# GpSimd's steady share of lower parts and sums given to VectorE in an attention + two-FFN kernel

## The chip, the cores and the metric

The kernel runs on one NeuronCore of a Trainium2 chip. The metric is device time in microseconds: the median of three timed runs. Five engines work side by side, each through its own instructions in the order in which they were written: TensorE (PE, matmul), VectorE (DVE), ScalarE (ACT), GpSimd (POOL) and SyncE (SP, which issues the DMAs here). GpSimd can't read PSUM, where matmuls leave their results; VectorE and ScalarE can.

## The reference

```python
def _attn_ref(q, k, v, mem_k, mem_v):          # 4 batches, 8 heads, 768 tokens, head_dim 64
    ...                                        # chunks of 32 queries see 8 memory keys and
    for c in range(nc):                        # their own window: 16 left, 32, 8 right
        ...
        scores = scale * np.matmul(q_c, k_full.transpose(0, 1, 3, 2))
        scores = scores - np.max(scores, axis=-1, keepdims=True)
        a = np.exp(scores)
        a = a / (np.sum(a, axis=-1, keepdims=True) + 1e-09)
        out[:, :, c_start:c_end] = np.matmul(a, v_full)
def _moe_ref(x, w_in, w_out):                  # 3072 tokens, 512 -> 2048 -> 512
    h = x @ w_in
    g = h * (1.0 / (1.0 + np.exp(-1.702 * h)))
    return (g @ w_out).astype(np.float32)
def _moe2_ref(x, w_gate, w_val, w_out):        # 512 -> 1536 -> 512
    g = x @ w_gate
    silu = g * (1.0 / (1.0 + np.exp(-g)))
    val = x @ w_val
    return (silu * val @ w_out).astype(np.float32)
```

Windowed attention, then a feed-forward network (FFN 1), then a gated one (FFN 2), all in float32.

## The kernel before

**Splitting.** Each float32 operand of a matmul is held as two numbers: an upper part (rounded to the type that TensorE takes, written by ScalarE: `split_hi`, L255 for weights, L432 for tokens, L561 for hidden values) and a lower part, what the rounding left (`split_lo`, L258 for weights, L436 for tokens, L565 for hidden values). A product is three matmul passes, `PASSES`: upper by upper, upper by lower, lower by upper. A lower part can be made only when its upper part is there.

**Seven products for eight.** A block of 512 tokens by 512 channels and the up-projection's weights are cut into 2 x 2 quarters, and sums of quarters are multiplied so that seven quarter products do for eight. Sums of weight quarters are `first_sums` and `second_sums` (L322, L323, L326, L327, 256 columns each); sums of token quarters are in `Tokens.sum` (L406, L409, L412, L415, 512 columns each). Each sum is then split too.

**Units.** A unit is one step along the hidden dimension for one block of tokens (`unit`, L465). PE runs, in this order: product 0 (into PSUM tile `ps_a`), product 1 (`ps_b`), a chunk of the down-projection of an earlier unit (`y`, L585), product 3 (`ps_a`), product 2 (`ps_c`, or the other half of `ps_b`), chunk 0, product 5 (`ps_a`), chunk 1, product 4 (`ps_c`), chunk 2, product 6 (`ps_a`); product 6 and the next unit's product 0 are neighbours. In FFN 2 a chunk is three matmuls of 512 columns, in FFN 1 six. A product is six matmuls of 256 columns. Between them ScalarE copies (L483, L492, L496) and VectorE adds (L487, L502, L508). After product 4 and L508 the activation of `ps_b` runs on ScalarE (L553 in FFN 2); after product 6 VectorE multiplies (L531 in FFN 2, L557 in part of FFN 1), ScalarE makes the upper part of the hidden values (L561) and VectorE the lower part (L565). Chunk 0 of the next unit reads it, in its second pass. Product 6 writes the PSUM tile that L502 reads and writes.

**Blocks.** There are 24 passes over a block, `seq`: six blocks with the first hidden units of FFN 1, six with the rest, then the same for FFN 2. At a change of block the next block's seven token operands are made during the last two units: `Tokens(..., TE)` has, for each of the 7 splits and 4 sums, the engine that does it. `EARLY`, `LATE` and `MAKE` say after which of the eleven places of a unit each is recorded; under `MAKE` operand 1 is split at place 0, behind product 0. At FFN 1's first five changes attention for the next block runs as well.

**Weights.** A generator, `weight_steps`, makes one unit's weight tiles in steps; `pace` (L954) takes a step or two at the places of a unit, in time for the unit's first use. A step is recorded on the engines at that place, so its instructions stand there in each engine's queue.

**Order.** The program for PE, ScalarE, VectorE and GpSimd runs as recorded (`manual_schedule`); only the order of SP's DMAs is chosen by a scheduler. The first part, up to the third unit of the second block, is an order written out by hand, `OPENING`.

Of the kernel before, what the change touches and what calls it, by code (L numbers as in the profile page):

```python
# [10 lines left out]
F32 = mybir.dt.float32  # L11
# [25 lines left out]
HALF = 2 * P  # L37
# [20 lines left out]
def tile_attention_moe_moe(  # L58
# [8 lines left out]
    nc = tc.nc  # L67
# [178 lines left out]
    def new_w(key):  # L246
        ring = max(rings, key=lambda r: r.room())
        wt[key], wslot[key] = ring.take()
# [5 lines left out]
    def split_hi(w, f, o=0, n=512):  # L254
        nc.scalar.copy(w[:, 0, o : o + n], f)  # L255

    def split_lo(w, f, o=0, n=512):
        nc.gpsimd.tensor_sub(w[:, 1, o : o + n], f, w[:, 0, o : o + n].bitcast(F32))  # L258

    def split_w(*a):  # L260
        split_hi(*a)
        split_lo(*a)

    raws = []
    AT = (0, 1, 4, 5, 2, 3, 6, 7)
# [40 lines left out]
    def next_weights(out):  # L306

        i = nraw[0]
        load_raw(i + RB)
        nraw[0] += 1  # L310
        take_words(i)
        yield 0
        shift_words(i)
        yield 0
        join_words(i)
        out += [bits.pop(i), raws[i]]

    def quarters(raw):
        return raw.bitcast(F32).rearrange("p (s n) -> p s n", s=4)

    def first_sums(s, a, b):
        nc.gpsimd.tensor_add(s[:, 0], b[:, :HALF], b[:, HALF:])  # L322
        nc.gpsimd.tensor_sub(s[:, 1], s[:, 0], a[:, :HALF])  # L323

    def second_sums(s, a, b):
        nc.gpsimd.tensor_sub(s[:, 2], a[:, :HALF], b[:, :HALF])  # L326
        nc.gpsimd.tensor_sub(s[:, 3], a[:, HALF:], s[:, 1])  # L327

    def weight_steps(ph, u):

        yield 0
        t = []
        yield from next_weights(t)
        a = t[0]
        yield 1
        new_w((ph, u, "a"))
        split_w(wt[ph, u, "a"], a)
        yield 0
        t = []
        yield from next_weights(t)  # L340
        b, raw = t
        s = quarters(raw)
        yield 0
        first_sums(s, a, b)
        yield 1 - u % 2
        if u % 2 == 0:
            new_w((ph, u, "v"))
        split_w(wt[ph, u - u % 2, "v"], b[:, HALF:], (u % 2) * HALF, HALF)
        yield 0
        second_sums(s, a, b)  # L350
        for i, n in enumerate(("s12", "s34")):
            yield 1
            new_w((ph, u, n))
            split_w(wt[ph, u, n], s[:, 2 * i : 2 * i + 2].rearrange("p s n -> p (s n)"))
        for o in range(OUTS[ph]):
            yield 0
            t = []
            yield from next_weights(t)
            yield 1
            new_w((ph, u, o))  # L360
            split_w(wt[ph, u, o], t[0])
        ready.add((ph, u))
# [3 lines left out]
    def all_weights():  # L366
        for ph in (1, 2):
            for u in range(2 * PLAIN if ph == 1 else 0, UNITS[ph]):
                yield from weight_steps(ph, u)
        yield None  # L370
# [67 lines left out]
    def load_tokens(src, engs):  # L438
        t = xpool.tile([P, KC, BLK], F32, tag="xf", name="xl")
        nc.sync.dma_start(out=t, in_=src)  # L440
        return Tokens(t, engs)
# [220 lines left out]
    V, G = nc.vector, nc.gpsimd  # L662
# [175 lines left out]
    def tokens():  # L838
# [27 lines left out]
        "ct": join_words,  # L866
        "wa": lambda u: new_split((1, u, "a"), bits[IN[u]]),
        "wal": lambda u: split_lo(wt[1, u, "a"], bits[IN[u]]),
        "sumA": lambda u: first_sums(*sums_of(u)),
        "sumB": lambda u: second_sums(*sums_of(u)),  # L870
        "wv": hi_v,
        "wvl": lambda u: split_v(u, split_lo),
        "wb": split_b,
        "wbl": lambda u: split_lo(wt[1, u, "a21"], bits[IN[u] + 1][:, :HALF], 0, HALF),
# [119 lines left out]
    LATE = {0: (-1, 0), 1: (-2, 1), 2: (-3,), 3: (3, -4), 4: (2,), 5: (5,), 7: (4,), 9: (6,)}  # L994

    pends = [None, None]
    TE = [V, G, V, G, V, G, V, G, V, V, G]
    done = 0
    for n, (ph, b, ua, ub) in enumerate(seq):
        nxt = seq[n + 1] if n + 1 < len(seq) else None  # L1000
# [5 lines left out]
        for u in range(ua, ub):  # L1006
# [4 lines left out]
            if last and attends and n:  # L1011
                tok = Tokens(xf.pop(nxt[1]), TE)
            places = PLACES[u - ua] if n > 1 and attends else ()
# [37 lines left out]
            if u == ua and nxt is not None and not attends:  # L1051
                src = {1: xd, 2: yd}[nxt[0]][nxt[1]]
                tok = load_tokens(src, TE)
            done += 1
# [53 lines left out]
```

## Time and profile before

| | |
|---|---|
| median of 3 runs | 1189.63 us (1189.48 to 1189.91) |
| the profiled execution's own time | 1190.33 us |
| its span in the profile | 1188.6 us |
| PE busy in the span | 97% |
| VectorE, ScalarE, GpSimd busy | 55%, 48%, 30% |

The profiled execution is 0.70 us above the median and 1.7 us longer than its span. Busy time is what the engine's instructions took; an engine that stands at an instruction whose input is not there yet is not busy, and everything behind that instruction waits too.

### The profile page before, as it was taken

To read this page: it belongs to the slowest core of one execution; us is meant where nothing else is said; L and a number is where in the kernel's file an instruction comes from. 1 tells how busy PE (TensorE), PEld (TensorE's weight loads), DVE (VectorE), ACT (ScalarE), POOL (GpSimd) and SP (SyncE) were. 2 spreads that over 40 slices of the span, in tenths; PEclk is the share of its full clock that TensorE was granted. 3 is DMA by queue.
4 is the path that set the end of the run, shared out by engine and by line. 5 is a ranking of instruction groups with operands and counts; after the bars stand their busy time and mean duration, and the time that the engine had idled before them with its cause. 6 is when DMAs were issued, how large, how long until landed. Compare 5 with 4: busy or idle time off the path is not lost.

```text
span 1188.6 us, 22301 instructions
## 1 busy us (share of the span) xinstructions
PE 1151.3 (97%) x8908; PEld 1039.6 (87%) x8908; DVE 652.1 (55%) x1117; ACT 568.1 (48%) x1185; POOL 354.9 (30%) x321
## 2 busy tenths in 40 slices
PE   4889999999999999999999999999999999999998
PEld 3778888888989999999988989999999999999997
DVE  5886756565765444443466564453556554453553
ACT  4866555455565454444455544343445544243342
POOL 4564221202454232321235433021345521021010
PEclk9889999999999999999999999999999999999999
DMA  9977354441454313322333321210225130320302
GB/s 304 296 253 231 110 157 120 130 140 63 137 166 118 106 66 114 131 74 62 106 116 107 106 99 36 72 71 1 89 89 178 36 103 5 107 92 15 107 25 83
DMA packets 62920, 131.47 MB, mean 111 GB/s; under 512 B 5728, under 2 KB 26208, under 8 KB 60512
## 3 DMA queue, kind: packets, MB, share of 16 engines
q1 hardware_dynamic: 62816, 130.05, 34.9%
q8 instruction: 70, 1.15, 0.4%
q14 instruction: 34, 0.28, 0.1%
HBM read 98.57 MB, written 31.46 MB: 109 GB/s over the span
## 4 chain that ended last, share of the span: by engine, by line
PE 86%; DMA 5%; DVE 3%; ACT 2%; issue 2%; POOL 1%; SPq 0%; DVEq 0%; ACTq 0%; POOLq 0%
PE y L585 35%; PE ps_a L450 27%; PE ps_c L450 12%; PE ps_b L450 9%; DMA raw<-in_wr 2%; PE ps_s L201 1%; PE ps_o L174 1%; DMA q<-in_qg 1%; DMA w<-in_kg 1%; DMA xd<-xf 1%; PE ps_t L158 1%; PE ps_v L174 1%; ACT ebd L167 0%; PE ps_u L546 0%; ACT g L551 0%
## 5 line engine op out<-in xcount | busy, mean ns | idle before, releaser
L450 PEld LDWEIGHTS ps_a<-b,w 128*128 128x128 f32 x2832 | 384.3, 189 | 39.6 <-DVE ps_a L502 4.2
L450 PE MATMUL ps_a<-b,w 128*128 128x256 f32 x2832 | 397.5, 283 | 5.7 <-DVE ps_a L502 2.1
L585 PE MATMUL y<-gs,w 128*128 128x512 f32 x1152 | 298.6, 395 | 0.6 <-DVE gs L565 0.5
L585 PE MATMUL y<-w,gs 128*128 128x512 f32 x864 | 247.7, 395 | 0.6 <-DVE gs L565 0.5
L585 PEld LDWEIGHTS y<-gs,w 128*128 128x128 f32 x1152 | 204.2, 189 | 36.2 <-DVE gs L565 1.4
L450 PE MATMUL ps_c<-b,w 128*128 128x256 f32 x1224 | 179.1, 282 | 0.0
L450 PEld LDWEIGHTS ps_c<-b,w 128*128 128x128 f32 x1224 | 167.1, 190 | 8.8
L585 PEld LDWEIGHTS y<-w,gs 128*128 128x128 f32 x864 | 144.2, 190 | 14.4 <-DVE gs L565 1.7
L258 POOL TENSOR_TENSOR w<-wf,w 128x512 fp32r<-128x512 f32 (+1 forms) x68 | 78.3, 1152 | 222.0 <-ACT w L255 221.9
L450 PE MATMUL ps_b<-b,w 128*128 128x256 f32 x900 | 135.5, 287 | 1.7 <-DVE ps_b L821 1.2
L450 PEld LDWEIGHTS ps_b<-b,w 128*128 128x128 f32 x900 | 120.4, 193 | 5.9 <-issue 1.7
L553 ACT ACTIVATE g<-ps_b 128x512 f32<-128x512 f32 x72 | 43.1, 598 | 166.1 <-DVE ps_b L508 166.1
L436 DVE TENSOR_TENSOR b<-xl,b 128x512 fp32r<-128x512 f32 x72 | 64.3, 893 | 80.4 <-ACT b L432 80.3
L502 DVE TENSOR_TENSOR ps_a<-m,ps_a 128x256 f32<-128x256 f32 x115 | 48.9, 426 | 104.0 <-PE ps_a L450 98.0
L492 ACT COPY u<-ps_a 128x256 f32<-128x256 f32 x115 | 43.0, 373 | 107.8 <-PE ps_a L450 107.6
L415 POOL TENSOR_TENSOR xl<-xl,t 128x512 f32<-128x512 f32 x18 | 23.3, 1296 | 231.3 <-DVE t L412 230.0
L565 DVE TENSOR_TENSOR gs<-ps_a,gs 128x512 fp32r<-128x512 f32 x118 | 80.8, 685 | 10.2 <-ACT gs L561 9.8
L487 DVE TENSOR_TENSOR ps_b<-p,ps_b 128x256 f32<-128x256 f32 x115 | 49.2, 427 | 61.3 <-PE ps_b L450 54.0
L561 ACT CAST gs<-ps_a 128x512 fp32r<-128x512 f32 x118 | 69.8, 592 | 22.5 <-DVE ps_a L531 15.6
L531 DVE TENSOR_TENSOR ps_a<-g,ps_a 128x512 f32<-128x512 f32 x72 | 50.0, 694 | 45.7 <-PE ps_a L450 45.2
L483 ACT COPY p<-ps_a 128x256 f32<-128x256 f32 x115 | 43.0, 374 | 60.3 <-PE ps_a L450 56.4
L508 DVE TENSOR_TENSOR ps_b<-u,ps_c 128x256 f32<-128x256 f32 x102 | 43.5, 426 | 50.1 <-PE ps_c L450 49.8
(123 smaller groups left out, 1190.6 us busy)
## 6 DMA issues: line engine op xcount, KB each, us to landing
raw<-in_wr SPq DMA_DIRECT2D x49, 512.0 KB, 3.4
xl<-yd SPq DMA_DIRECT2D x12, 1024.0 KB, 4.8
vm<-in_vg SPq DMA_DIRECT2D x22, 512.0 KB, 6.0
kbd<-in_kg SPq DMA_DIRECT2D x32, 256.0 KB, 4.2
raw<-in_wr SPq DMA_DIRECT2D x30, 256.0 KB, 5.3
yp<-o SPq DMA_DIRECT2D x24, 256.0 KB, 3.8
xl<-xd SPq DMA_DIRECT2D x6, 1024.0 KB, 4.8
base<-yp SPq DMA_DIRECT2D x24, 256.0 KB, 3.4
```

What stands on the lines that cost most here:

```text
L258: nc.gpsimd.tensor_sub(w[:, 1, o : o + n], f, w[:, 0, o : o + n].bitcast(F32))
L436: self.engs[k].tensor_sub(x[:, 1], self.source(k), x[:, 0].bitcast(F32))
L450: nc.tensor.matmul(ps, w[:, a, o + kc * P : o + kc * P + P], x[:, c, kc, :], start=(start and kc == 0 and (a, c) == PASSES[0]), stop=(kc = ...
L483: nc.scalar.copy(p1, ca[:, :n])
L487: add(cb[:, :n], p1, cb[:, :n])
L502: add(ca[:, n:], m, ca[:, :n])
L508: add(cb[:, n:], u2, cc)
L531: late[0] = [lambda: nc.vector.tensor_mul(ca, t, ca), lambda: gs.append(cast(ca))]
L553: nc.scalar.activation(t, c, AF.Silu)
L561: nc.scalar.copy(x[:, 0], g)
L565: nc.vector.tensor_sub(x[:, 1], g, x[:, 0].bitcast(F32))
L585: nc.tensor.matmul(y, lhs, rhs, start=(first and o == 0 and (a, c) == PASSES[0]), stop=(ends and o == len(gs) - 1 and (a, c) == passes[-1]),)
```

## The change

VectorE takes, outside the written first part, the lower parts of weights, the sums of weight quarters, and those token splits and sums that GpSimd had. ScalarE's upper parts stay, and so does the place at which each piece is recorded.

```diff
-    def split_lo(w, f, o=0, n=512):
-        nc.gpsimd.tensor_sub(w[:, 1, o : o + n], f, w[:, 0, o : o + n].bitcast(F32))
+    def split_lo(w, f, o=0, n=512, eng=nc.gpsimd):
+        eng.tensor_sub(w[:, 1, o : o + n], f, w[:, 0, o : o + n].bitcast(F32))
     def split_w(*a):
         split_hi(*a)
-        split_lo(*a)
+        split_lo(*a, eng=nc.vector)
...
-    def first_sums(s, a, b):
-        nc.gpsimd.tensor_add(s[:, 0], b[:, :HALF], b[:, HALF:])
-        nc.gpsimd.tensor_sub(s[:, 1], s[:, 0], a[:, :HALF])
+    def first_sums(s, a, b, eng=nc.gpsimd):
+        eng.tensor_add(s[:, 0], b[:, :HALF], b[:, HALF:])
+        eng.tensor_sub(s[:, 1], s[:, 0], a[:, :HALF])
...
-        first_sums(s, a, b)
+        first_sums(s, a, b, nc.vector)
...
-        second_sums(s, a, b)
+        second_sums(s, a, b, nc.vector)
...
-    TE = [V, G, V, G, V, G, V, G, V, V, G]
+    TE = [V] * 11
```

(`second_sums` gets the same argument as `first_sums`.) 258 instructions move from GpSimd's queue to VectorE's: 84 of L258, 66 of L436, 22 each of L406 and L415, 16 each of L322, L323, L326 and L327. 178 of them have 512 columns and 80 have 256. The orders of PE and of ScalarE are the same as before; a few DMAs of SP change places with their neighbours.

VectorE's queue at a change of block in FFN 2 with no weight step near (`ps_a_10570` is the last unit but one, `ps_b_10677` the last; `b` are token operands):

```order
 L531 TENSOR_TENSOR ps_a_10570<-g_10641,ps_a_10570 128x512
+L436 TENSOR_TENSOR b_10674<-xl_10117,b_10674 128x512
 L487 TENSOR_TENSOR ps_b_10677<-p1_10660,ps_b_10677 128x256
 L565 TENSOR_TENSOR gs_10672<-ps_a_10570,gs_10672 128x512
+L436 TENSOR_TENSOR b_10689<-t2_10621,b_10689 128x512
 L436 TENSOR_TENSOR b_10707<-xl_10117,b_10707 128x512
+L436 TENSOR_TENSOR b_10713<-t3_10600,b_10713 128x512
 L502 TENSOR_TENSOR ps_a_10663<-m_10662,ps_a_10663 128x256
```

The lower part of operand 1 now stands ahead of L487 and L565; those of operands 3 and 5 stand behind L565 and ahead of L502.

VectorE's queue at an earlier change of block in FFN 2, with a weight tile `w` split at the last place of the unit before:

```order
 L508 TENSOR_TENSOR ps_b_7118<-u2_7105,ps_c_7141 128x256
 L301 SCALAR_TENSOR_TENSOR wf_7172<-raw_6966,wf_7172 128x512
+L258 TENSOR_TENSOR w_7197<-wf_7172,w_7197 128x512
 L531 TENSOR_TENSOR ps_a_7107<-g_7185,ps_a_7107 128x512
+L436 TENSOR_TENSOR b_7214<-xl_7006,b_7214 128x512
 L487 TENSOR_TENSOR ps_b_7217<-p1_7200,ps_b_7217 128x256
 L565 TENSOR_TENSOR gs_7212<-ps_a_7107,gs_7212 128x512
```

Here the weight's lower part stands ahead of L531 as well.

VectorE's queue one block later, where one unit's weight sums (in `raw`) and the tiles made of them are recorded:

```order
 L301 SCALAR_TENSOR_TENSOR wf_7282<-raw_7092,wf_7282 128x512
+L322 TENSOR_TENSOR raw_7092<-wf_7282 128x256
+L323 TENSOR_TENSOR raw_7092<-raw_7092,wf_7172 128x256
+L258 TENSOR_TENSOR w_7346<-wf_7282,w_7346 128x256
 L502 TENSOR_TENSOR ps_a_7299<-m_7298,ps_a_7299 128x256
 L609 TENSOR_SCALAR o_7359<-y1_7072 128x512
+L326 TENSOR_TENSOR raw_7092<-wf_7172,wf_7282 128x256
+L327 TENSOR_TENSOR raw_7092<-wf_7172,raw_7092 128x256
 L508 TENSOR_TENSOR ps_b_7310<-u2_7297,ps_c_7330 128x256
+L258 TENSOR_TENSOR w_7373<-raw_7092,w_7373 128x512
+L258 TENSOR_TENSOR w_7388<-raw_7092,w_7388 128x512
 L531 TENSOR_TENSOR ps_a_7299<-g_7371,ps_a_7299 128x512
```

Two sums now stand ahead of L508, and two weight tiles' lower parts between L508 and L531. This piece occurs twice in FFN 2.

## Rows read from the trace of the kernel before

**Rows 1.** Windows: stretch, then busy us (instructions) of PE, PEld, DVE, ACT, POOL.
```profile
620.00:720.00 100.00, 98.58 (x673) 90.14 (x672) 57.23 (x98) 50.69 (x108) 45.47 (x44) 1.00 0.28 98
720.00:880.00 160.00, 160.00 (x1110) 149.34 (x1109) 76.39 (x139) 67.00 (x145) 33.67 (x31) 1.00 0.17 60
...
120.00:1160.00 1040.00, 1034.36 (x7395) 940.39 (x7394) 555.44 (x959) 486.18 (x1018) 292.46 (x257) 1.00 0.30 93
```

**Rows 2.** Timeline, FFN 2 change of block with weights: start, us, engine, line.
```profile
885.77 0.68 DVE L409 TENSOR_TENSOR xl<-xl 128x512 f32<-128x512 f32 x1
...
887.16 1.29 POOL L258 TENSOR_TENSOR w<-wf,w 128x512 fp32r<-128x512 f32 x1 [2.32 <-ACT w L255]
887.21 1.79 DVE L412 TENSOR_TENSOR t<-t,xl 128x512 f32<-128x512 f32 x1
...
888.92 0.41 DVE L502 TENSOR_TENSOR ps_a<-m,ps_a 128x256 f32<-128x256 f32 x1
...
889.39 1.69 PE L450 MATMUL ps_a<-b,w 128*128 128x256 f32 x12 [0.31 <-DVE ps_a L502]
```

**Rows 3.** Timeline, VectorE, at another change of block in FFN 2.
```profile
691.79 1.78 DVE L301 SCALAR_TENSOR_TENSOR wf<-raw,wf 128x512 int32<-128x512 int32 x1
```

**Rows 4.** Timeline of the quiet change of block in FFN 2.
```profile
956.20 0.43 DVE L487 TENSOR_TENSOR ps_b<-p,ps_b 128x256 f32<-128x256 f32 x1 [0.73 <-PE ps_b L450]
956.22 0.64 ACT L432 CAST b<-xl 128x512 fp32r<-128x512 f32 x1
956.54 0.68 DVE L565 TENSOR_TENSOR gs<-ps_a,gs 128x512 fp32r<-128x512 f32 x1
...
956.94 1.30 POOL L436 TENSOR_TENSOR b<-xl,b 128x512 fp32r<-128x512 f32 x1 [2.21 <-ACT b L432]
...
958.07 0.86 PE L585 MATMUL y<-w,gs 128*128 128x512 f32 x3
...
958.77 0.87 PE L450 MATMUL ps_a<-b,w 128*128 128x256 f32 x6
```

**Rows 5.** Timeline, FFN 2: a chunk 0 that waited for L565.
```profile
649.73 0.69 DVE L565 TENSOR_TENSOR gs<-ps_a,gs 128x512 fp32r<-128x512 f32 x1 [0.32 <-ACT gs L561]
649.76 0.48 PE L585 MATMUL y<-w,gs 128*128 128x512 f32 x1
...
651.04 0.86 PE L450 MATMUL ps_a<-b,w 128*128 128x256 f32 x6
```

**Rows 6.** Timeline of a token sum and L565 in FFN 1 with attention.
```profile
176.10 0.69 DVE L409 TENSOR_TENSOR xf<-xf 128x512 f32<-128x512 f32 x1 [1.64 <-DMA xd<-xf]
176.71 0.68 DVE L565 TENSOR_TENSOR gs<-ps_a,gs 128x512 fp32r<-128x512 f32 x1
...
177.45 0.73 PE L585 MATMUL y<-gs,w 128*128 128x512 f32 x2 [0.51 <-DVE gs L565]
```

**Rows 7.** Timeline, FFN 2 change of block with a weight tile.
```profile
639.49 0.62 ACT L255 CAST w<-wf 128x512 fp32r<-128x512 f32 x1
...
641.98 0.86 PE L585 MATMUL y<-w,gs 128*128 128x512 f32 x3
```

**Rows 8.** Timeline, FFN 2: the weight sums and what is made of them.
```profile
653.35 0.43 DVE L508 TENSOR_TENSOR ps_b<-u,ps_c 128x256 f32<-128x256 f32 x1
...
654.30 0.61 ACT L255 CAST w<-raw 128x512 fp32r<-128x512 f32 x1
...
654.82 0.70 DVE L531 TENSOR_TENSOR ps_a<-g,ps_a 128x512 f32<-128x512 f32 x1 [1.04 <-PE ps_a L450]
...
655.30 0.62 ACT L255 CAST w<-raw 128x512 fp32r<-128x512 f32 x1
...
658.11 0.86 PE L585 MATMUL y<-w,gs 128*128 128x512 f32 x3
```

**Rows 9.** Timeline at the change from the first half of FFN 1 to its second.
```profile
324.84 0.60 ACT L551 ACTIVATE g<-ps_b 128x512 f32<-128x512 f32 x1 [4.50 <-DVE ps_b L508]
...
328.15 0.98 PE L450 MATMUL ps_a<-b,w 128*128 128x256 f32 x6 [0.84 <-ACT p L483]
```

More of the change, by code (lines that the diff above doesn't have):

```diff
@@ L319, in quarters, with second_sums @@
         return raw.bitcast(F32).rearrange("p (s n) -> p s n", s=4)
-    def first_sums(s, a, b):
-        nc.gpsimd.tensor_add(s[:, 0], b[:, :HALF], b[:, HALF:])
-        nc.gpsimd.tensor_sub(s[:, 1], s[:, 0], a[:, :HALF])
-    def second_sums(s, a, b):
-        nc.gpsimd.tensor_sub(s[:, 2], a[:, :HALF], b[:, :HALF])
-        nc.gpsimd.tensor_sub(s[:, 3], a[:, HALF:], s[:, 1])
+    def first_sums(s, a, b, eng=nc.gpsimd):
+        eng.tensor_add(s[:, 0], b[:, :HALF], b[:, HALF:])
+        eng.tensor_sub(s[:, 1], s[:, 0], a[:, :HALF])
+    def second_sums(s, a, b, eng=nc.gpsimd):
+        eng.tensor_sub(s[:, 2], a[:, :HALF], b[:, :HALF])
+        eng.tensor_sub(s[:, 3], a[:, HALF:], s[:, 1])
     def weight_steps(ph, u):
```

## The prediction

> **What bounds the kernel now.** I read the windows by stage first. From 120 to 1160 us PE is idle for 1040.00 - 1034.36 = 5.64 us in all [rows 1]. Where few weights are made, from 720 to 880 us, it has no idle time: PE is the floor there, and a faster VectorE buys nothing. So an upper limit on the gain stands at once, about 5.6 us or 0.5%; the downside has no such limit. What idle time there is lies where weights and block changes meet, as from 620 to 720 us (1.42 us), and in the first blocks of FFN 1. The second view is the timeline around those idle times, because PE waits there for one VectorE or ScalarE instruction, and the question for each is what stands ahead of it in its queue.
>
> **Work moved.** GpSimd takes 1.29 us for a lower part of 512 columns, VectorE 0.68 us for the same shape [rows 2], and 0.43 us for 256 columns [rows 4]. The 178 and 80 moved instructions come to 178 x 0.68 + 80 x 0.43 = 155 us, which lifts VectorE from 555 us to at most 710 of 1040 us, 68% [rows 1]. On average that fits. As GpSimd isn't waited for except through its results, its 292 us saved are worth nothing by themselves; what counts is where the 258 instructions stand in VectorE's queue.
>
> **What gets better.** VectorE and GpSimd get in each other's way: L409 took 0.68 us alone, and the like L412 took 1.79 us beside a GpSimd instruction that ran from 887.16 to 888.45 [rows 2]. That made L502 late, and PE waited for it (0.31 us idle at 889.39). With GpSimd silent L412 is 1.1 us shorter; one lower part of 0.60 us takes its place ahead of L502, so L502 ends 0.5 us earlier: gain 0.5. At 691.79 us a contended L301 of 1.78 us stands ahead of another late L502 [rows 3], and one lower part is added: 0.5 again. By the same steps I put the remaining late L502 and L531 of FFN 2 at 0.6 together, since what is added there eats most of the relief. The largest is in FFN 1: contended instructions hold L508 back, ScalarE stands 4.50 us for it, and PE then waits 0.84 us for ScalarE's copy [rows 9]. Without contention L508 comes 1.2 us earlier; the pause and its restart are worth 1.1. Sum of gains 0.5 + 0.5 + 0.6 + 1.1 = 2.7 us; bounds 1 and 5.64.
>
> **What gets worse, 1: quiet block changes of FFN 2.** Before, operand 1's lower part ran on GpSimd at 956.94 while VectorE did L487 and L565 [rows 4]. Now it stands ahead of both, and waits for ScalarE's upper part, which ends at 956.22 + 0.64 = 956.86. Back to back, an instruction of 512 columns holds the next one up by 0.61 us (176.10 to 176.71 [rows 6]), one of 256 columns by 0.34 (956.20 to 956.54 [rows 4]). So L436 starts at 956.86, L487 at 957.47, L565 at 957.81 and ends at 958.49, against 957.22 before. When must it end? At 649 us L565 ended at 650.42, 0.66 us after chunk 0 began, and the next product came 1.28 us after that begin [rows 5] where 0.70 is normal (958.07 to 958.77 [rows 4]): 0.58 us lost, so L565 is free up to 0.08 us behind the chunk's begin. Here it ends 0.42 behind: 0.34 us lost. FFN 2 has eleven block changes; nine look like this one (the one at 688 us too), 9 x 0.33 = 3.0 us. Bounds: 0 where the upper part gets ready 0.34 us sooner, 0.6 if semaphores add half of that again. The operands behind L565 delay L502 by some 0.5 us, which has 1.2 us to spare: nothing.
>
> **Worse, 2: the two other block changes.** Near 640 us a weight tile's lower part stands ahead of L531 too. ScalarE writes its upper part until 639.49 + 0.62 = 640.11 [rows 7]. L531 then starts at 640.7 instead of 639.5; ScalarE's conversion of the hidden values follows at 641.4, operand 1's upper part behind it at about 641.9 to 642.6, its lower part from 642.6, L487 at 643.2, L565 from 643.55 to 644.2. Chunk 0 began at 641.98: 2.1 us late. VectorE's chain ahead of this is up to 0.6 us faster without GpSimd, so 1.5 is my value, with 0.9 and 2.1 as ends. Near 892 us the weight tile stands behind L565 and only operand 1 is ahead; by the same steps 0.7 (0.3 to 1.3), since the chain is later there than in the quiet case.
>
> **Worse, 3: weight sums ahead of L508.** At 653 us L326 and L327 and a late L502 push L508 from 653.35 to about 654.1 [rows 8]. ScalarE's activation follows 0.74 us late, and so do the two upper parts behind it, which ended at 654.91 and 655.92. The second lower part then starts at 656.7, L531 at 657.3 instead of 654.82, the conversion ends at 658.6, L565 at 659.3. Chunk 0 began at 658.11: 1.1 us lost. If ScalarE weren't late, L531 would start at 656.55 and 0.45 would be lost. The pattern comes twice (at 907 us again): 2 x 1.0 = 2.0 us, ends 0.9 and 2.3. Other weight steps stand behind L565, or ahead of L531 with the one unit's slack of about 0.9 us that the quiet case shows between L565's end and chunk 0's begin [rows 4]: nothing, and 0.3 us each for some ten of them if that slack is gone.
>
> **Worse, 4: FFN 1 with attention.** At 176.10 us L409 had waited for a store to DRAM that reads the same tile, L565 stood behind it, and PE behind L565 [rows 6]. Operand 1's lower part now stands between the two: 0.61 us more for PE. This pattern comes twice: 1.2 us, ends 0.6 and 1.3. In the rest of FFN 1 chunks are twice as long and I count nothing.
>
> **Sum.** Costs 3.0 + 1.5 + 0.7 + 2.0 + 1.2 = 8.4 us, gains 2.7, net +5.7 us. The profiled execution would go from 1190.33 to about 1196.0 us; it stands 0.70 above the median, so the median goes from 1189.63 to **1195.3 us**.
>
> **Rivals.** No difference is what lies within 0.2%, or 2.4 us: about what a measurement of this kernel can tell.
>
> *Relief wins (faster).* Every idle time of PE that contention causes goes, and the new waits are shorter than I work out, because ScalarE, too, gets its inputs earlier. For it speaks that the sums were on the path of the upper parts made from them; against it, that the quiet change has no contention ahead of it and still comes out 0.34 us late. Gains alone: 1189.63 - 2.7 = 1186.9 us; the floor is 1189.63 - 5.64 = 1184.0. It decides if operand 1's lower part is done 0.34 us sooner than I have it. The Trainium skill, "GPSIMD Engine Reference", section "4.1 Engine selection", says that elementwise work on a tile belongs on VectorE, about twice as fast as GpSimd for two inputs. By that rule this change is a gain, and the time would be this rival's 1186.9 us. The trace agrees on the ratio (1.29 to 0.68 us), but not on what follows from it, as GpSimd's speed isn't what PE waits for. Chance 0.07.
>
> *A draw.* The terms with weight tiles (1.5, 0.7 and 2.0) don't appear, since VectorE catches up; the quiet changes and the attention (4.2) stay against gains of 2.7: 1189.63 + 1.5 = 1191.1 us. Chance 0.18.
>
> *ScalarE and VectorE in lockstep (much slower).* Every one of the 84 + 66 lower parts makes VectorE stand until ScalarE's queue has reached its upper part, ScalarE then stands for VectorE's next result, and the slack of ordinary units goes. 84 weight tiles at 0.15 us would add 12.6 us to my sum: 1207.9 us. Against it: VectorE is idle more than 40% of both windows of FFN 2 [rows 1], and most weight steps stand where ScalarE has nothing else ahead. Chance 0.10.
>
> **How the numbers follow.** My forecast (1192 to 1202, around 1195.3) has the remaining 0.65. The range leaves out about one in ten on each side: 1190.0 to 1201.0, from the draw's lower part up to all costs at their upper ends with the gains halved (8.4 + 4 - 1.4 = 11). Faster by over 0.2%: 0.07; within: 0.18; slower: 0.65 + 0.10 = 0.75.
>
> **What would show it.** The profile of the changed kernel has GpSimd idle after about 120 us, VectorE near 66% busy from 120 to 1160 us, and no L409, L412, L301 or L296 above 0.9 us there. PE's new idle time stands at chunk 0 (L585) and is put down to L565: once in each block change of FFN 2, about 0.3 us, and around 1 us at the two units behind the weight sums. The waits of PE for L502 near 692 and 889 us and for the copy near 328 us are gone. I'm wrong if PE's idle time doesn't grow, if it stands ahead of products and not of chunk 0, or if matmuls themselves change pace.

## The result: 0.7% slower, and where it went

The changed kernel takes 1198.78 us (median of 4 runs, 1195.43 to 1200.29) against 1189.77 us before: ratio 1.0069, 95% interval 1.0057 to 1.0082. Ratios are taken from fast runs alone and need not equal the quotient of two medians (1.0076 here); one run each of experiments 6 and 8, with 3762.56 and 1600.19 us, is left out of them. The profiled execution took 1199.83 us, its span is 1198.0 us. The page's busy times and three windows (columns as in [rows 1]):

```profile
PE 1155.7 (96%) x8908; PEld 1040.2 (87%) x8908; DVE 748.2 (62%) x1375; ACT 570.8 (48%) x1185; POOL 59.4 (5%) x63
...
620.00:720.00 100.00, 96.90 (x656) 88.23 (x655) 72.40 (x141) 49.96 (x105) 0.00 (x0) 1.00 0.30 101
720.00:880.00 160.00, 159.68 (x1103) 148.28 (x1103) 89.31 (x167) 66.83 (x142) 0.00 (x0) 1.00 0.17 60
120.00:1160.00 1040.00, 1029.57 (x7341) 933.30 (x7340) 648.24 (x1209) 486.29 (x1015) 0.00 (x0) 1.00 0.29 92
```

PE's idle time in the long window goes from 5.64 us [rows 1] to 10.43, although the matmuls are the same and the granted clock is full (1.00); as the kernel is slower, 54 fewer of them fall into the window. VectorE is busy 648 of 1040 us, 62%: it isn't short of time. PE's own waits from 120 to 1175 us (total, times, longest) say what PE waits for, first in the changed kernel, then in the kernel before:

```profile
PE y L585 <- DVE gs L565: 5.7, 8, 1.7
PE ps_a L450 <- DVE ps_a L502: 1.5, 3, 0.9
PE ps_o L174 <- ACT ebd L167: 1.3, 3, 0.5
...
PE ps_a L450 <- DVE ps_a L502: 2.1, 5, 0.6
...
PE ps_a L450 <- ACT p L483: 1.1, 2, 0.8
PE y L585 <- DVE gs L565: 1.0, 3, 0.5
```

So waits ahead of products shrank (though the longest for L502 grew from 0.59 to 0.92 us, at 960.69 us), those of its matmuls for L483's copy are gone, and the wait of chunk 0 for the hidden values' lower part grew.

To size each place I took, from both traces, the start of product 1 of 116 units from 106 us on, and how much the distance to the kernel before grows from one unit to the next. (The sums of idle time say less than the starts, since the ends of matmuls are modelled and some records are missing.)

| place | predicted | found |
|---|---|---|
| eight quiet block changes of FFN 2 | 8 x 0.33 = 2.6 | 0.35 to 0.39 at seven, 0.55 at one: 3.15 |
| the change near 691 us, and the unit behind it | 0.33 - 0.5 = -0.2 | 0.59 - 0.88 = -0.3 |
| change near 640 us, and the units beside it | 1.5 - 0.6 = 0.9 | 1.94 - 0.30 - 0.56 = 1.1 |
| change near 892 us, and the units beside it | 0.7 - 0.5 = 0.2 | 0.74 - 0.64 - 0.16 = -0.1 |
| weight sums at 655 and 907 us | 2 x 1.0 = 2.0 | 1.33 + 1.32 = 2.65 |
| attention at 176 and 230 us | 2 x 0.6 = 1.2 | 1.15 + 0.30 = 1.45 |
| FFN 1 near 325 us | -1.1 | -0.73 |
| sum | 5.7 | 7.2 |

The distance at the last unit is 9.0 us in these two executions; the spans differ by 9.4, so 0.4 us more stand behind it. Of the 9.0, small steps elsewhere add 0.1, and another 1.7 us stand ahead of the first of these units (106.3 us before, 108.0 now): in the written opening, where every engine's order is the same in both kernels.

The quiet change of block that answers to [rows 4], in the timeline of the changed kernel:

```profile
961.14 0.42 DVE L508 TENSOR_TENSOR ps_b<-u,ps_c 128x256 f32<-128x256 f32 x1
...
963.44 0.62 ACT L432 CAST b<-xl 128x512 fp32r<-128x512 f32 x1
...
964.09 0.69 DVE L436 TENSOR_TENSOR b<-xl,b 128x512 fp32r<-128x512 f32 x1 [1.17 <-ACT b L432]
...
964.70 0.42 DVE L487 TENSOR_TENSOR ps_b<-p,ps_b 128x256 f32<-128x256 f32 x1
965.03 0.69 DVE L565 TENSOR_TENSOR gs<-ps_a,gs 128x512 fp32r<-128x512 f32 x1
965.07 0.39 PE L585 MATMUL y<-w,gs 128*128 128x512 f32 x1
...
965.77 0.73 PE L585 MATMUL y<-w,gs 128*128 128x512 f32 x2 [0.31 <-DVE gs L565]
...
966.35 0.86 PE L450 MATMUL ps_a<-b,w 128*128 128x256 f32 x6
```

VectorE stands 1.17 us idle at L436 until ScalarE's upper part is there, with L487 and L565 behind it. Chunk 0's first pass runs, its second waits. From 965.07 to the next product it is 1.28 us, where 0.70 is normal: 0.58 us. This is the one change of the eight that cost 0.55 from unit to unit. L415, a token sum that ran on GpSimd before, stands ahead of L508 here (960.54 us, 0.69 long), and L508 comes 0.59 us late (961.14, against 953.55 and units that are 7.00 us later). With it ScalarE's upper part comes 0.22 us later than worked out. At the other seven all of the loss, too, stands at chunk 0.

The change of block with a weight tile, which stood near 640 us in the kernel before, in the changed kernel:

```profile
641.47 0.62 ACT L255 CAST w<-wf 128x512 fp32r<-128x512 f32 x1
...
642.12 0.69 DVE L258 TENSOR_TENSOR w<-wf,w 128x512 fp32r<-128x512 f32 x1 [0.69 <-ACT w L255]
...
642.73 0.69 DVE L531 TENSOR_TENSOR ps_a<-g,ps_a 128x512 f32<-128x512 f32 x1
...
644.59 0.69 DVE L436 TENSOR_TENSOR b<-xl,b 128x512 fp32r<-128x512 f32 x1 [1.17 <-ACT b L432]
...
645.53 0.69 DVE L565 TENSOR_TENSOR gs<-ps_a,gs 128x512 fp32r<-128x512 f32 x1
```

Two waits for ScalarE stand one behind the other in VectorE's order, L258's ahead of L531 and L436's ahead of L565. The loss at chunk 0 is 2.0 us. And the unit with the weight sums, which answers to [rows 8]:

```profile
657.02 0.42 DVE L326 TENSOR_TENSOR raw<-wf 128x256 f32<-128x256 f32 x1
657.36 0.42 DVE L327 TENSOR_TENSOR raw<-wf,raw 128x256 f32<-128x256 f32 x1
...
657.69 0.42 DVE L508 TENSOR_TENSOR ps_b<-u,ps_c 128x256 f32<-128x256 f32 x1
658.15 0.60 ACT L553 ACTIVATE g<-ps_b 128x512 f32<-128x512 f32 x1 [2.43 <-DVE ps_b L508]
...
659.28 0.69 DVE L258 TENSOR_TENSOR w<-raw,w 128x512 fp32r<-128x512 f32 x1 [1.17 <-ACT w L255]
...
660.15 0.38 ACT L483 COPY p<-ps_a 128x256 f32<-128x256 f32 x1
660.29 0.69 DVE L258 TENSOR_TENSOR w<-raw,w 128x512 fp32r<-128x512 f32 x1 [0.31 <-ACT w L255]
660.58 0.77 PEld L450 LDWEIGHTS ps_a<-b,w 128*128 128x128 f32 x6 [0.57 <-ACT p L483]
660.90 0.69 DVE L531 TENSOR_TENSOR ps_a<-g,ps_a 128x512 f32<-128x512 f32 x1
...
663.16 0.73 PE L585 MATMUL y<-w,gs 128*128 128x512 f32 x2 [0.41 <-DVE gs L565]
```

L508 is held up 0.67 us by two sums, and L531 by two lower parts that wait for ScalarE. The unit loses at two places. With L508 all of ScalarE's queue is late, L483's copy too, and the weight loads of product 3 wait for that copy: 0.4 us are lost ahead of chunk 0. At chunk 0 another 0.9 are lost, first to L561 and then to L565. In FFN 1, what answers to [rows 6] and [rows 9]:

```profile
178.41 0.69 DVE L409 TENSOR_TENSOR xf<-xf 128x512 f32<-128x512 f32 x1 [1.78 <-DMA xd<-xf]
179.02 0.68 DVE L436 TENSOR_TENSOR b<-xf,b 128x512 fp32r<-128x512 f32 x1
179.62 0.68 DVE L565 TENSOR_TENSOR gs<-ps_a,gs 128x512 fp32r<-128x512 f32 x1
...
180.36 0.73 PE L585 MATMUL y<-gs,w 128*128 128x512 f32 x2 [1.62 <-DVE gs L565]
...
327.37 0.60 ACT L551 ACTIVATE g<-ps_b 128x512 f32<-128x512 f32 x1 [3.56 <-DVE ps_b L508]
```

The lower part of operand 1 stands between L409 and L565 as worked out, and PE's wait grows from 0.51 to 1.62 us. Near 327 us ScalarE stands 3.56 us for L508 instead of 4.50.

### The profile page after: what moved, and what is told of

It is laid out like the page before. It is cut to its first block, busy times and chain, and to the rows that moved or that the text cites. A ratio compares the mean times of both kernels' runs of the same rounds, so it can differ in the third digit from the quotient of the medians.

```text
span 1198.0 us, 22056 instructions
## 1 busy us (share of the span) xinstructions
PE 1155.7 (96%) x8908; PEld 1040.2 (87%) x8908; DVE 748.2 (62%) x1375; ACT 570.8 (48%) x1185; POOL 59.4 (5%) x63
## 3 DMA queue, kind: packets, MB, share of 16 engines
q8 instruction: 70, 1.15, 0.4%
## 4 chain that ended last, share of the span: by engine, by line
PE 83%; DVE 5%; DMA 4%; ACT 4%; issue 2%; POOL 0%; SPq 0%; DVEq 0%; ACTq 0%
PE y L585 35%; PE ps_a L450 26%; PE ps_c L450 11%; PE ps_b L450 8%; DMA raw<-in_wr 2%; DMA vm<-in_vg 2%; PE ps_s L201 1%; PE ps_o L174 1%; DVE gs L565 1%; PE ps_u L546 1%; DMA xd<-xf 1%; ACT gs L561 1%; ACT b L432 1%; ACT w L255 0%; ACT ebd L167 0%
## 5 line engine op out<-in xcount | busy, mean ns | idle before, releaser
L585 PE MATMUL y<-w,gs 128*128 128x512 f32 x864 | 250.5, 397 | 4.6 <-DVE gs L565 3.8
L436 DVE TENSOR_TENSOR b<-xl,b 128x512 fp32r<-128x512 f32 x90 | 62.2, 691 | 60.3 <-ACT b L432 59.3
L502 DVE TENSOR_TENSOR ps_a<-m,ps_a 128x256 f32<-128x256 f32 x115 | 48.9, 425 | 76.7 <-PE ps_a L450 75.9
L565 DVE TENSOR_TENSOR gs<-ps_a,gs 128x512 fp32r<-128x512 f32 x118 | 80.9, 685 | 8.1 <-ACT gs L561 8.0
L561 ACT CAST gs<-ps_a 128x512 fp32r<-128x512 f32 x118 | 69.6, 590 | 26.4 <-DVE ps_a L531 16.2
L487 DVE TENSOR_TENSOR ps_b<-p,ps_b 128x256 f32<-128x256 f32 x115 | 49.1, 427 | 39.2 <-PE ps_b L450 36.3
L483 ACT COPY p<-ps_a 128x256 f32<-128x256 f32 x115 | 42.9, 373 | 61.3 <-PE ps_a L450 58.0
L531 DVE TENSOR_TENSOR ps_a<-g,ps_a 128x512 f32<-128x512 f32 x72 | 49.9, 694 | 34.7 <-PE ps_a L450 33.2
L508 DVE TENSOR_TENSOR ps_b<-u,ps_c 128x256 f32<-128x256 f32 x102 | 43.7, 428 | 39.5 <-PE ps_c L450 38.7
L432 ACT CAST b<-xl 128x512 fp32r<-128x512 f32 x90 | 55.9, 621 | 8.0 <-PE ps_a L450 7.8
L603 DVE SCALAR_TENSOR_TENSOR base<-y,base 128x512 f32<-128x512 f32 x48 | 32.9, 691 | 34.9 <-PE y L585 34.1
```

The lines of the kernel that those rows point to most:

```text
L432: nc.scalar.copy(self.ops[k][:, 0], self.source(k))
L436: self.engs[k].tensor_sub(x[:, 1], self.source(k), x[:, 0].bitcast(F32))
L483: nc.scalar.copy(p1, ca[:, :n])
L487: add(cb[:, :n], p1, cb[:, :n])
L502: add(ca[:, n:], m, ca[:, :n])
L508: add(cb[:, n:], u2, cc)
```

## The experiments

Two theories. **Queue (mine):** what costs time is what stands ahead of L565, L531 and L508 in VectorE's order; the number of instructions on VectorE doesn't matter. **Load (rival):** VectorE has too many instructions and waits, wherever they stand. Behind them a third, **contention**: two-input instructions of GpSimd and VectorE hold each other up, and its end is what the change gains. All times are medians; each ratio is to the kernel before on the same chip (1189.45 to 1189.8 us there).

**1. Operand 1 later.** The changed kernel with operand 1 split behind the chunk that follows product 1, where operand 3 is, so that L487 and L565 are ahead of it: two places later under `MAKE`, one under `LATE`, the table of the attention blocks.

```diff
-    MAKE = {0: (1,), 2: (3,), 4: (2,), 5: (5,), 7: (4,), 9: (6,)}
-    LATE = {0: (-1, 0), 1: (-2, 1), 2: (-3,), 3: (3, -4), ...
+    MAKE = {2: (1, 3), 4: (2,), 5: (5,), 7: (4,), 9: (6,)}
+    LATE = {0: (-1, 0), 1: (-2,), 2: (1, -3), 3: (3, -4), ...
```

> All on VectorE as in the change, but token operand 1 is split one place later, behind L565, not ahead of it. Theory A (the cost is what stands ahead of L565 and L531 in VectorE's queue): the nine quiet block changes give back about 0.37 us each (3.3), the one near 640 us some 1.9, the one near 892 us some 0.5, the two in the attention part 1.4 together: about 7 us less than the change, 1192 us, and no chunk 0 of a quiet block change waits for L565. Rival B (the cost is VectorE's load and the number of its waits for ScalarE, wherever they stand): both are the same as in the change, so 1198 to 1199 us.

1191.34 us, ratio 1.0016 (1.0007 to 1.0025). Of the 9.0 us lost, 7.4 are back, with every instruction still on VectorE. Its timeline at the quiet change:

```profile
956.44 0.43 DVE L487 TENSOR_TENSOR ps_b<-p,ps_b 128x256 f32<-128x256 f32 x1 [0.27 <-PE ps_b L450]
956.69 0.62 ACT L432 CAST b<-xl 128x512 fp32r<-128x512 f32 x1
956.83 0.69 DVE L565 TENSOR_TENSOR gs<-ps_a,gs 128x512 fp32r<-128x512 f32 x1
...
957.43 0.68 DVE L436 TENSOR_TENSOR b<-xl,b 128x512 fp32r<-128x512 f32 x1
```

L436 waits for nothing now, and L565 ends at 957.52, ahead of chunk 0 (958.31). In the starts of units nothing is left at the quiet changes, 640 us costs 0.72 instead of 1.94, the attention block at 176 us gains 0.79 instead of losing 1.15, and 655 and 907 us still cost 1.33 and 1.37. Not all of this is the place: at 176 us the store that L409 waits for took 3.60 us from issue to landing here, 4.98 in the changed kernel and 4.48 before, which makes 1.4 of the 7.1 us between the two traces from 172 us on. The place is worth the other 5.7, about what experiment 7 gives. The load theory falls here: VectorE is as busy as in the changed kernel (651 us of 1040).

**2. Second weight sums back on GpSimd.** The changed kernel, with L326 and L327 where they were.

```diff
-        second_sums(s, a, b, nc.vector)
+        second_sums(s, a, b)
```

> As the change, but second_sums (L326, L327) stay on GpSimd. Theory A: L508 isn't held up where the weight sums of FFN 2 stand ahead of it (two places, 1.3 us each), so about 2.3 us less than the change, 1196.5 us, with some contention back. Rival B: 32 of 258 instructions and 14 of 155 us go back, a tenth of the loss: 0.8 us less, 1198 us.

1196.20 us, ratio 1.0069 (1.0055 to 1.0083): by the ratio no different from the change. In the trace the two units cost 0.91 and 0.76 instead of 1.33 and 1.32. At 655 us product 3 is on time and the loss stands at chunk 0 alone, so the part ahead of chunk 0 was the sums'. The direction is the queue theory's, the 1 us in all is below what five runs could tell.

**3. Tokens alone, and 4. weights alone.** The two halves of the change.

```diff
 # 3: the kernel before, with
-    TE = [V, G, V, G, V, G, V, G, V, V, G]
+    TE = [V] * 11
 # 4: the changed kernel, with
-    TE = [V] * 11
+    TE = [V, G, V, G, V, G, V, G, V, V, G]
```

> Only the token splits and sums go to VectorE (110 of the 258 instructions); weights stay on GpSimd. Theory A: the quiet block changes (3.3 us) and the attention part (1.4) cost as in the change, part of the relief (1 to 2 us) comes: plus 3.5 us, 1193.3 us. Rival B: 75 of 155 us moved, so half of the loss: plus 4.5 us, 1194.3 us, and the idle time of PE spread over units and not at the block changes.

> Only the weights' lower parts and sums go to VectorE (148 of the 258 instructions); tokens as before. Theory A: 2.6 us at the two places behind the weight sums, little at the one near 640 us, relief of 1 to 2 us: plus 1 us, 1190.8 us; no loss at quiet block changes. Rival B: 80 of 155 us moved, half of the loss: plus 4.6 us, 1194.4 us.

Tokens: 1194.09 us, 1.0044 (1.0031 to 1.0056). The total lies between the two forecasts and nearer to the load theory's (1194.3), but the steps are where the queue theory has them: 0.35 to 0.39 at the quiet changes (0.57 at the one shown above), 1.13 and 0.61 with attention, nothing at 655 and 907 us. One more, 0.58 at 955 us, where PE waits 0.91 us for L502, neither theory had. Weights: 1194.33 us, 1.0050 (1.0037 to 1.0063). Here my number (1190.8) failed, and the load theory's (1194.4) came out. By totals alone these two runs would speak for it; the steps don't, nor do experiments 1, 7 and 8, in which the same instructions cost less at other places. No loss stands at the quiet changes, so the rival's spread isn't there either; but the units at 640, 649, 655 and 907 us cost 0.92, 0.69, 1.99 and 1.36. The 1.99 has a row of its own:

```profile
653.79 1.44 POOL L406 TENSOR_TENSOR t<-xl 128x512 f32<-128x512 f32 x1 [7.86 <-DMA xl<-yd]
653.99 1.52 DVE L327 TENSOR_TENSOR raw<-wf,raw 128x256 f32<-128x256 f32 x1
655.43 0.41 DVE L508 TENSOR_TENSOR ps_b<-u,ps_c 128x256 f32<-128x256 f32 x1
```

A token sum on GpSimd runs beside a weight sum on VectorE, which takes 1.52 us where it takes 0.42 with GpSimd silent, and L508 is behind it. Half a change brings all of its queue losses and leaves the contention.

**5. Weights' lower parts later, on VectorE.** Experiment 1, and each weight's lower part goes into a list that is recorded at the next of the places 2 to 8, before the next raw words are taken, or when the next unit needs it.

```diff
     def split_w(key, *a):
         split_hi(*a)
-        split_lo(*a, eng=nc.vector)
+        owed.append((key, a))
+    def pay(key=None):
+        if key is None or any(k == key for k, _ in owed):
+            for _, a in owed:
+                split_lo(*a, eng=nc.vector)
+            owed.clear()
...
             def after(i):
+                if 2 <= i <= 8:
+                    pay()
...
```

> As the run with operand 1 later, and each weight's lower part is recorded some places later on VectorE, behind the product or the activation that VectorE serves at that place. The queue theory (what stands ahead of L531 and L508 in VectorE's order sets the loss): the step at the 640 us unit (+0.7 in the run with operand 1 later) goes, and of the two at 655 and 907 us (+1.3 each) the part that the lower parts make, about half; relief at 325, 692 and the attention blocks stays. 1191.3 - 0.7 - 1.3 = about 1189.3 us, range 1188.3 to 1190.3, no slower than the kernel before. The load theory (the number of instructions on VectorE counts, not their place): as the run with operand 1 later, 1191.3 us, within 0.5.

**1186.91 us, ratio 0.9978 (0.9969 to 0.9987)**: faster than both kernels, and than I expected. Its timeline at the weight sums (lines behind L258 are 9 higher: L517 is L508, L540 is L531, L574 is L565):

```profile
651.08 0.42 DVE L517 TENSOR_TENSOR ps_b<-u,ps_c 128x256 f32<-128x256 f32 x1
651.53 0.60 ACT L562 ACTIVATE g<-ps_b 128x512 f32<-128x512 f32 x1 [2.29 <-DVE ps_b L517]
652.03 0.61 ACT L255 CAST w<-raw 128x512 fp32r<-128x512 f32 x1
652.16 0.70 DVE L540 TENSOR_TENSOR ps_a<-g,ps_a 128x512 f32<-128x512 f32 x1 [0.67 <-ACT g L562]
...
654.89 0.68 DVE L574 TENSOR_TENSOR gs<-ps_a,gs 128x512 fp32r<-128x512 f32 x1
...
655.49 0.68 DVE L258 TENSOR_TENSOR w<-raw,w 128x512 fp32r<-128x512 f32 x1
```

L531 follows the activation at once and L258 has gone behind L565. The two units cost 0.27 and 0.29 instead of 1.33 and 1.32, all of it ahead of chunk 0 at 655 us, 640 us costs nothing and 892 us 0.33; the gains (1.10 near 325 us, 0.58 near 692, 0.56 near 889) stay.

**6. The same, second sums on GpSimd.** Experiment 5 with the edit of experiment 2.

> As the run with later lower parts, and the second pair of weight sums (L326 and L327, 16 each) goes back to GpSimd. The queue theory: the two sums no longer stand ahead of L508 at 655 and 907 us, which is worth some 0.4 us at each; GpSimd's 32 instructions bring little contention back. 1188.5 us, range 1187.5 to 1189.7. If the sums aren't on the path or contention takes the gain: as that run or up to 1 us slower.

1187.12 us, 0.9975 (0.9966 to 0.9984): the same as 5, so the gain that the queue theory expected didn't come. The units at 655 and 907 us cost 0.23 and 0.28 there. That doesn't show that the two sums cost nothing, because L517 (L508) is no earlier without them:

```profile
648.62 0.84 DVE L332 TENSOR_TENSOR raw<-raw,wf 128x256 f32<-128x256 f32 x1
...
649.72 0.85 DVE L258 TENSOR_TENSOR w<-wf,w 128x256 fp32r<-128x256 f32 x1
...
651.09 0.41 DVE L517 TENSOR_TENSOR ps_b<-u,ps_c 128x256 f32<-128x256 f32 x1
```

Beside GpSimd's sums two instructions ahead of it take 0.84 and 0.85 us, and 0.43 and 0.42 in experiment 5. Contention has taken the place of the sums.

**7. Tokens alone with operand 1 later.** Experiment 3 with the edit of experiment 1.

> Weights stay on GpSimd; tokens' lower parts and sums are all on VectorE, and operand 1 is made at the later place. The queue theory: the losses of the tokens' part stood at block changes, ahead of L487 and L565, and go with the place: 1194.1 - 9 x 0.35 - 1.7 (attention) = about 1189.2 us, range 1188 to 1190.5. The load theory: as the run with the tokens alone, 1194.1 us, since the same 110 instructions are on VectorE.

1188.23 us, 0.9990 (0.9981 to 0.9998). The place is worth 5.9 us here too, and this half alone is no slower than the kernel before.

**8. Weights at the later places, tokens still shared.** Experiment 5 with the `TE` of the kernel before.

> Weights' lower parts and sums on VectorE, recorded at the later places, operand 1 at its later place; GpSimd keeps its share of the tokens. The queue theory: the steps of the run with the weights alone at 640, 649, 655 and 907 us (+0.9, +0.7, +2.0, +1.4) go: 1194.3 - 4.5 = about 1189.8 us, or a little less. The contention theory (the tokens' work on GpSimd, beside VectorE's weights, made most of that loss): 1192 us or more.

1190.30 us, 1.0003 (0.9994 to 1.0012). 4.0 us of the 4.9 that the weights cost are back. At 655 us 1.09 stays (0.27 in experiment 5), which goes with the contention seen in experiment 4: the same weight sum takes 1.52 us there again, beside a GpSimd sum of 1.35.

**9. The places alone.** The kernel before, with the later places of experiment 5 for the work that stays on GpSimd.

> The engines as before the change (GpSimd has its share), but operand 1 and the weights' lower parts at the later places. If the better time of the run with both later on VectorE comes from VectorE having the work in a harmless order: no gain here, 1189.6 us, or up to 2 us slower since GpSimd's parts come later. If it comes from the places alone: about 1187 us here too.

1189.84 us, 1.0001 (0.9992 to 1.0010). The places bring nothing by themselves: on GpSimd these instructions stood ahead of nothing that PE waits for. Between this kernel and experiment 5 only the engine differs, so at these places VectorE is worth 2.9 us.

**10. GpSimd doing the work a second time.** Experiment 1, where GpSimd also works out the weights' lower parts and every second operand's, into a tile that nobody reads, 256 columns at a time.

```diff
     def split_w(*a):
         split_hi(*a)
         split_lo(*a, eng=nc.vector)
...
+        for j in range(0, n, HALF):
+            nc.gpsimd.tensor_sub(shadow, f[:, j : j + HALF], w[:, 0, off + j : off + j + HALF].bitcast(F32))
...
```

> As the run with operand 1 later, and GpSimd works out the weights' lower parts and every second operand's lower part a second time, in 256-column pieces, into a scratch tile that nobody reads; nothing waits for it but the reuse of its inputs' buffers. The contention theory (GpSimd's and VectorE's two-input instructions hold each other up, and its absence is what the change gains): L409, L412 and L301 beside it take over 1 us again, the gains at 325, 692 and in the attention go, and the time is 1191.3 + about 3 = 1194.3 us, range 1193 to 1196.5. If GpSimd's work beside VectorE costs nothing: 1191.3 us, within 0.5.

1229.11 us, 1.0324 (1.0310 to 1.0338): a loss of 38 us over experiment 1 where I expected 3. Part of it may be that operands' buffers are given back only when GpSimd is done, hence:

**11. The same load on a tile of GpSimd's own.** It reads one column of the upper part and then works on its own tile (against experiment 10).

```diff
+        nc.gpsimd.tensor_copy(trig, w[:, 0, off : off + 1].bitcast(F32))
         for j in range(0, n, HALF):
-            nc.gpsimd.tensor_sub(shadow, f[:, j : j + HALF], w[:, 0, off + j : off + j + HALF].bitcast(F32))
+            nc.gpsimd.tensor_sub(shadow, shadow, shadow)
...
```

> As the run with the shadow on GpSimd, but GpSimd reads one column of each upper part and then runs its 256-column two-input instructions on a tile of its own alone: it no longer holds the operands' and the words' buffers for as long as it works. The contention theory: the instructions of VectorE beside them still take over 1 us (L436 0.9 us on average or more), and the time stays far above that of the run with operand 1 later, at 1215 to 1232 us. The buffer theory (the shadow's loss came from buffers given back late): L436 is back near 0.7 us, or is long without effect, and the time falls to 1191 to 1196 us.

1211.98 us, 1.0179 (1.0163 to 1.0195). The time lies between the two forecasts: 17 of the 38 us were tied to the shared operands, and 21 remain with none shared but for the one column. VectorE's groups from 120 to 1160 us in this run (L577 is L565, L444 is L436):

```profile
L577 DVE TENSOR_TENSOR gs<-ps_a,gs 128x512 fp32r<-128x512 f32 x110 | 75.4, 686 | 9.3 <-ACT gs L573 9.1
L444 DVE TENSOR_TENSOR b<-xl,b 128x512 fp32r<-128x512 f32 x86 | 72.3, 840 | 32.2 <-ACT b L440 32.0
...
L444 DVE TENSOR_TENSOR b<-t,b 128x512 fp32r<-128x512 f32 x42 | 42.5, 1011 | 2.9 <-ACT b L440 2.9
```

and in experiment 1, with GpSimd silent:

```profile
L436 DVE TENSOR_TENSOR b<-xl,b 128x512 fp32r<-128x512 f32 x90 | 62.0, 689 | 44.4 <-ACT b L432 44.2
...
L436 DVE TENSOR_TENSOR b<-t,b 128x512 fp32r<-128x512 f32 x44 | 30.2, 686 | 3.1 <-ACT b L432 3.1
```

The third number from the bar is mean ns. L436 reads two tiles of SBUF and grows from 0.69 to 0.84 and 1.01 us; L565, which reads one of SBUF and one of PSUM, keeps its 0.686. The Trainium skill, "GPSIMD Engine Reference", section "8. Key points", says that GpSimd shares its SBUF interfaces with VectorE and contends with VectorE's instructions that have two SBUF inputs or run in a 2-port mode. The rows agree for two inputs. Why GpSimd's load costs so much more here than its 292 us did before isn't separated: it starts with VectorE's lower part of the same data each time, which it seldom did before, but that is argued and not tried.

## Why the prediction was right, by its steps

**Forecast.** 1195.3 us, 1190.0 to 1201.0, was 3.5 us short of the median and held it. Costs and gains were both larger than worked out: the table's costs come to 10.5 us for 8.4, its gains to 3.3 for 2.7, so 0.6 of the miss cancelled. The places make 7.2 us for the 5.7 (0.5 of it a store's time, see Attention); the rest of the distance is no place that I had worked out.

**Quiet block changes.** Right in mechanism and place, and in size at seven of nine: 0.35 to 0.39 for 0.33. The change that I worked out line by line [rows 4] is not one of them: it cost 0.55, since the token sum ahead of L508 delayed the upper part, which I had not counted. The one at 688 us cost 0.59, and its gains 0.88, so that the right sum there is partly luck. Experiment 1 shows the cause by taking it away.

**640 us.** Right: the chain ahead gained 0.30 and the change of block itself cost 1.94, together 1.64 for my 1.5. Another 0.56 came back a unit later, at the wait of [rows 5], which I had under the rest of FFN 2's gains (0.6).

**892 us.** The 0.74 is the 0.7 worked out; the gains beside it were 0.8 and not 0.5.

**Weight sums.** Mis-sized, 1.33 for 1.0, and right in place only in part: at 655 us 0.9 stand at chunk 0, where I had 1.0, but another 0.4 ahead of it, where product 3 waits for L483's copy. I had made ScalarE late and left that copy out. (The 0.45 us for the case with ScalarE on time leave out the 0.08 that the quiet case allows; with them it is 0.36.) Of the two causes I named, the lower parts ahead of L531 make the larger share by themselves: without the sums 0.91 and 0.76 stay (experiment 2), without the lower parts 0.27 and 0.29 (experiment 5). An L508 that is 0.6 us late, as in experiments 5 and 6, thus costs about 0.3 us by itself, whether sums or contention make it late.

**Attention.** Right in mechanism, and in size near 176 us. There the 1.15 are the 0.6 for L436 and 0.50 because the store that L409 waits for took 4.98 us from issue to landing instead of 4.48. That store takes 3.60 to 5.02 us in the traces, and the step follows it: with operand 1 at the old place on VectorE it is 0.6 plus what the store takes beyond 4.48 (experiments 2 and 3: 0.03 with 3.90 us, 1.13 with 5.02). At 230 us the place is worth about 0.5 (0.36 in experiment 2, -0.17 in experiment 7, with stores of 3.78 us in both); why the step there is 0.30 in the change isn't separated.

**Gains.** L301 and L412 are at 0.68 us; PE's waits for L502 near 692 and 889 us and for L483's copy near 328 us are gone, as forecast. FFN 1 gave 0.73 for 1.1; it gives 1.10 with the lower parts later (experiment 5), and also with the second sums on GpSimd (experiment 2).

**VectorE's load.** I had at most 710 us, 68%; it is 648, 62%. The instructions that GpSimd had stretched became shorter (L436's mean from 0.91 to 0.69 us, L296's from 0.60 to 0.42), and instructions back to back overlap in the records (0.68 us long, 0.61 apart), which the 155 us don't allow for.

**Rivals.** The draw (0.18) needed VectorE to catch up at the weight tiles, which it did nowhere but near 892 us. Lockstep (0.10) would have shown at ordinary units; behind the first few none of them moved by over 0.15 us. The rule of the Trainium skill, "GPSIMD Engine Reference", section "4.1 Engine selection" (elementwise work belongs on VectorE), gave 1186.9 us by the relief rival. The change as written contradicts it; experiment 5, the same work on the same engine in another order, reaches 1186.91. Equal figures are partly chance, but the step that the rule leaves out is the order.

**Not foreseen, and open.** The opening. Its program is unchanged, and yet the first unit starts between 1.90 us earlier than in the kernel before (experiment 3) and 1.70 us later (the change), so I take it for variation from one execution to the next; it belongs to the spread of the changed kernel's four runs, 4.9 us. Between medians and traces there is a further difference. In the change and in experiments 1, 2, 4, 10 and 11, the kernels with the weights' lower parts on VectorE at the old places, the median stands 1.8 to 2.3 us further from the kernel before than the units from 172 us on do in the traces (the change: 9.0 against 7.2). Much of that is the choice of the first unit. These six, and only these, also lose 0.3 us or more near 141 us, gain 0.2 near 157 and lose 0.3 to 0.5 near 172. Counted from the end of the opening (117 us), with the 0.4 us behind the last unit and with the store at 176 us set to its time in the kernel before, 1.4 us are left for the change and 0.9 for experiment 4, and at most 0.6 either way for every other one. What makes up the 1.4 isn't shown.

## What to carry to other kernels

Moving work to an engine that is faster and has time to spare can still cost: an in-order queue makes whatever stands behind the moved instruction wait for the moved instruction's inputs too. So place each moved instruction behind what the bottleneck engine needs next: here the places were worth about 11 us (1198.78 to 1186.91, by the ratios 0.9%), and turned a loss of 0.7% into a gain of 0.2%. Judge a half of such a move by itself only with care, since the half that stays keeps the contention.

## What the runs showed of the hardware that I had not expected

- What GpSimd's two-input work beside VectorE's costs doesn't follow from its time: 275 us of it on a tile of its own, whose results nothing waits for, made the kernel 20.6 us slower (experiment 11 against 1), while the 292 us that the kernel before had cost about 2.9 us at the later places (experiment 9 against 5). What makes the difference isn't shown.
- A two-input instruction of VectorE of 256 columns took 1.52 us beside a GpSimd sum of 1.44 us, 1.1 more than its 0.42, nearly the whole length of the other (experiment 4).
- Two inputs are not needed for that: L296, which reads one tile of SBUF, took 1.45 us beside a GpSimd sum (637.07 us in the kernel before), and 0.42 on average with GpSimd silent.
- The same store to DRAM of attention's results, issued at the same place of its unit, took 3.60 to 5.02 us to land in the traces of these kernels.
- The same written opening ended up to 3.6 us apart in executions of kernels that don't differ there (granted clock over the first 120 us: 0.91 before, 0.90 in the change, 0.93 in experiment 5).
